# Group 0's first q and k loaded as FP32 by SyncE and cast on ScalarE and VectorE, with the first pass laid out anew

## The chip, the cores and the metric

The kernel runs on one core of a Trainium2 chip. The metric is the device time of one execution in microseconds. The engines are called as in the profile: PE (TensorE, matrix products), PEld (its weight loads), DVE (VectorE), ACT (ScalarE), POOL (GpSimd) and SP (SyncE). Loads and stores are DMA transfers. POOL and SP each issue them on a queue of their own; a load that changes the type on its way (FP32 in the chip's main memory, FP16 in its on-chip memory) is issued by POOL.

## The reference

Sigmoid attention, followed by a gated two-layer network without a bias:

```python
batch, n_heads, seq, head_dim = (8, 12, 448, 64)
scores = scale * np.matmul(q, k.transpose(0, 1, 3, 2)) - np.log(S)
attn = 1.0 / (1.0 + np.exp(-scores))
attn_out = np.matmul(attn, v)
...
x = attn_out.transpose(0, 2, 1, 3).reshape(B * S, H * D)     # 3584 x 768
h = x @ w_in                                                # 768 x 2048
g = h * (1.0 / (1.0 + np.exp(-beta * h)))
return (g @ w_out)                                          # 2048 x 768
```

q, k and v are FP32, as are the weights and the output.

## The kernel before, in words

**Groups.** Four heads of one batch make a group: 24 groups, three to a batch (`QPB`). For a group, `load_one` (L122) brings q or k into a tile `raw` of 128 partitions (32 for each head) with 14 chunks of 64 elements per partition, as FP16. `transpose` (L201) turns it on DVE into `qT` (L207) or `kT` (L216 for 12 chunks, L220 for the last two). There are three `raw` tiles, so the loads of group 3 write where group 0 was.

**Attention.** `score` (L230) is a matmul of 32 rows; two of them (e = 0, 1) accumulate a piece of the scores in PSUM. For batch 0 the scores are made in half visits (`half_visit`, L294): 224 query columns, with the key tiles 0 and 1 (`second` = 0) or 2 and the rest (`second` = 1). A visit writes two score tiles, and there are three of those in rotation (`share_psum(3)`), two pairs later on. ACT takes the sigmoid (L249, or L264 for two tiles in one instruction) into `attns`. `attend` (L316) multiplies with v (L334) and DVE casts the result into `xT` (L343). The v rows beyond the third key tile are loaded on their own (`load_v_last`) and copied once on DVE for the other half of the heads (`double_v_last`, L171).

**Network.** `dense1` multiplies batch 0 and 1 with w_in (L356), takes the sigmoid on ACT (L368) and the product on DVE into `gt` (L371), a tile of 128 x 16 x 896 FP16. `dense2` multiplies with w_out (L386). Later batches use products of sums of blocks (L510 and L628), which are not touched here.

**Order.** Each engine runs its instructions in the order in which the program writes them. The first pass (batch 0) is written out by hand: a list `LOADS` of loads on POOL's queue, a function `loads` with the ones after it, and a list `BEGIN` of steps: `q` and `k` are transposes, `scores` a half visit (group, half, second), `values` an `attend`, `dense` so many matmuls of the network (`fill_units`), `beta` four small transposes of beta, `idle` so many matmuls of a tile of zeros (`still`, L751), whose result nobody reads. `two` changes the score tiles from three pairs to two. After `BEGIN` a planner spreads the network's matmuls over the visits of the other groups.

**Start.** POOL issues the load of the first half of q of group 0 (chunks 0 to 6) and of its whole k, ahead of two small memsets; ACT runs a sigmoid of one column (`dummy`, L742) once its table is loaded; DVE sets `still` and `beta_in` to zero; PE runs 11 zero matmuls; SP issues the small load of beta (L766); POOL goes on with `LOADS`.

Of the kernel before, what the change touches and what calls it, by code (L numbers as in the profile page):

```python
# [8 lines left out]
FP32 = mybir.dt.float32  # L9
FP16 = mybir.dt.float16  # L10
# [3 lines left out]
def kernel(  # L14
# [10 lines left out]
    nc = tc.nc  # L25
# [3 lines left out]
    B, H, S, D = q.shape  # L29
    NTOK, DM = out.shape  # L30
    DFF = moe_w_in.shape[1]
    P = 128
    BLK = 32
    HQ = P // BLK
    NB = S // BLK
# [19 lines left out]
    rawp = ctx.enter_context(tc.tile_pool(name="rawp", bufs=3))  # L55
# [29 lines left out]
    def bank(cols: int = S, hold=None, at=None):  # L85
        if at is None:
            at = min((i for i in used if i not in held.values()), key=used.get)
        assert at not in held.values()
        touch(at)
        if hold is not None:  # L90
            held[hold] = at
        width[at] = cols
        return ps[:, at, 0:cols]
# [25 lines left out]
    raws = {}  # L119
    vs = {}  # L120

    def load_one(g: int, r: int, c0: int = 0, c1: int = NB):  # L122
        b, t = divmod(g, QPB)
        if g not in raws:
            raws[g] = rawp.tile([P, 2, NB, D], FP16, tag="raw", name="raw")
        nc.gpsimd.dma_start(  # L126
            out=raws[g][:, r, c0:c1].rearrange("p c d -> p (c d)"),
            in_=(q, k)[r][b, HQ * t : HQ * (t + 1)].rearrange("h (p c) d -> (h p) (c d)", c=NB)[
                :, c0 * D : c1 * D
            ],  # L130
        )

    def load_qk(g: int):
        load_one(g, 0)
        load_one(g, 1)
# [7 lines left out]
    def load_v_full(b: int, lo: int = 0, hi: int = H):  # L143

        if b not in vs:
            vs[b] = vp.tile([P, H, JF + 1, D], FP16, tag="v16", name="v16")
        rows = v[b, lo:hi].rearrange("h (p c) d -> p h (c d)", c=NB)
        for i in range(HQ):
            nc.gpsimd.dma_start(
                out=vs[b][i * BLK : (i + 1) * BLK, lo:hi, 0:JF].rearrange("p h j d -> p h (j d)"),  # L150
                in_=rows[:, :, JF * i * D : JF * (i + 1) * D],
            )
            ready.update((b, "full", t, i) for t in range(lo // HQ, hi // HQ))

    def load_v_last(b: int):
        if b not in vs:
            vs[b] = vp.tile([P, H, JF + 1, D], FP16, tag="v16", name="v16")
        rows = v[b].rearrange("h (p c) d -> p h c d", c=NB)
        for c in range(NF, NB):
            lo = (c - NF) * BLK  # L160
            nc.gpsimd.dma_start(out=vs[b][lo : lo + BLK, :, JF], in_=rows[:, :, c])
        ready.add((b, "last"))

    def load_v(b: int):
        load_v_full(b)
        load_v_last(b)

    def double_v_last(b: int):
        assert (b, "last") in ready
        ready.add((b, "v"))  # L170
        nc.vector.tensor_copy(out=vs[b][KL:P, :, JF], in_=vs[b][0:KL, :, JF])  # L171
# [3 lines left out]
    def load_w_in(lo: int, hi: int):  # L175

        nc.gpsimd.dma_start(
            out=w_in16[:, :, lo * P : hi * P],
            in_=moe_w_in[:, lo * P : hi * P].rearrange("(c p) f -> p c f", p=P),
        )  # L180

    def load_w_out(c: int, half: int):
        n = NDC // WOUT
        cols = slice(half * HALF, (half + 1) * HALF)
        nc.gpsimd.dma_start(
            out=w_out16[:, c * n : (c + 1) * n, cols],
            in_=moe_w_out[c * n * P : (c + 1) * n * P, cols].rearrange("(c p) f -> p c f", p=P),
        )
# [5 lines left out]
    ready = set()  # L194


    def in_order(b: int, t):
        t = t.rearrange("p c e -> p (c e)").bitcast(FP32)
        return t.rearrange("p (q c) -> p c q", c=NB) if b == B - 1 else t

    def transpose(g: int, r: int, c0: int = 0, c1: int = NB):  # L201
        raw = raws[g][:, r]
        if r == 0:
            if g not in qT:
                qT[g] = qTp.tile([P, NB * BLK, PAIR], FP16, tag="qT", name="qT")
            ready.update((g, "q", c) for c in range(c0, c1, NB // 2))
            nc.vector.transpose(  # L207
                out=in_order(g // QPB, qT[g][:, c0 * BLK : c1 * BLK]),
                in_=raw[:, c0:c1].rearrange("p c d -> p (c d)").bitcast(FP32),
            )  # L210
            return
        ready.add((g, "k"))
        kT[g] = kTp.tile([P, S, PAIR], FP16, tag="kT", name="kT")
        to = kT[g].rearrange("p k e -> p (k e)").bitcast(FP32)
        frm = raw.rearrange("p c d -> p (c d)").bitcast(FP32).rearrange("p (c f) -> p c f", c=NB)
        nc.vector.transpose(  # L216
            out=to[:, 0 : JF * P].rearrange("p (j i q) -> p i j q", j=JF, i=HQ),
            in_=frm[:, 0:NF].rearrange("p (i j) f -> p i j f", j=JF),
        )
        nc.vector.transpose(  # L220
            out=to[:, JF * P :], in_=frm[:, NF:].rearrange("p c f -> p (c f)")
        )
# [123 lines left out]
    gt = const.tile([P, NDC, WIN], FP16, name="gt")  # L346
# [388 lines left out]
    NH = NB // 2  # L735
    share_psum(3)
    with tc.manual_schedule():
        load_one(0, 0, 0, NH)
        load_one(0, 1)
        nc.gpsimd.memset(nlogs, NEG_LOG_S)  # L740
        nc.gpsimd.memset(dummy, 0.0)
        nc.scalar.activation(out=dummy, in_=dummy, func=AF.Sigmoid, bias=0.0, scale=1.0)  # L742
# [4 lines left out]
        idle = bank(512)  # L747

        def idle_units(n: int):
            for _ in range(n):  # L750
                nc.tensor.matmul(idle, still[:, 0:P], still, start=True, stop=True)  # L751

        idle_units(11)
        def load(what, *a):
            if what == "q":
                load_one(a[0], 0, a[1] * NH, (a[1] + 1) * NH)
            elif what == "k":
                load_one(a[0], 1)
            elif what == "v":
                load_v_full(0, a[0] * HQ, a[1] * HQ)  # L760
            elif what == "last":
                load_v_last(0)
            elif what == "w_in":
                load_w_in(*a)

        nc.sync.dma_start(out=beta_in[0:NDC], in_=moe_beta.rearrange("(c p) -> c p", p=P))  # L766
        LOADS = [
            ("q", 1, 0), ("k", 1), ("q", 2, 0), ("k", 2), ("last",), ("v", 0, 3), ("q", 0, 1), ("q", 1, 1),
            ("w_in", 0, 2), ("w_in", 2, 4), ("q", 2, 1), ("w_in", 4, 6), ("w_in", 6, 8), ("w_in", 8, 10),
            ("w_in", 10, 12), ("w_in", 12, 14), ("w_in", 14, 16),  # L770
        ]
        for x in LOADS:
            load(*x)

        def loads():
            load_qk(3)
            load_w_out(0, 0)
            load_w_out(1, 0)
            load_v(1)
            load_qk(4)  # L780
            load_qk(5)
            load_w_out(0, 1)
            load_w_out(1, 1)

        def beta_columns():
            ready.add("beta")
# [2 lines left out]
                nc.vector.transpose(out=beta_sb[part], in_=beta_in[:, part])  # L789

        BEGIN = [
            ("q", 0, 0), ("k", 0), ("q", 1, 0), ("scores", 0, 0, 1), ("idle", 4), ("k", 1), ("idle", 4),
            ("scores", 0, 0, 0), ("k", 2), ("q", 2, 0), ("scores", 1, 0, 0), ("idle", 4), ("v", 0),
            ("scores", 1, 0, 1), ("scores", 2, 0, 0), ("values", 0, 0), ("q", 0, 1), ("q", 1, 1),
            ("scores", 2, 0, 1), ("beta",), ("values", 1, 0), ("scores", 0, 1, 0), ("values", 2, 0),
            ("scores", 0, 1, 1), ("loads",), ("q", 2, 1), ("dense", 12), ("scores", 1, 1, 1), ("two",),
            ("dense", 6), ("scores", 1, 1, 0), ("dense", 18), ("scores", 2, 1, 0), ("values", 0, 1),
            ("values", 1, 1), ("scores", 2, 1, 1), ("dense", 9), ("values", 2, 1), ("dense", 42), ("k", 3),
            ("q", 3, 0), ("q", 3, 1), ("dense", 21),
        ]  # L800
        for what, *a in BEGIN:
            if what == "q":
                g, half = a
                transpose(g, 0, half * NH, (half + 1) * NH)
            elif what == "k":
                transpose(a[0], 1)
            elif what == "scores":
                half_visit(a[0], a[1] * QH, a[2])
            elif what == "idle":
                idle_units(a[0])  # L810
            elif what == "v":
                double_v_last(a[0])
            elif what == "values":
                attend(a[0], a[1] * QH, QH, a[2:] or (0, 1))
            elif what == "dense":
                fill_units(a[0])
            elif what == "beta":
                beta_columns()
            elif what == "loads":
                loads()  # L820
            elif what == "two":
                share_psum(2)
# [143 lines left out]
```

## Time and profile before

Three runs took 376.13, 376.32 and 376.49 us.

| | us |
|---|---|
| median of the runs | 376.32 |
| the profiled execution's own time | 376.51 |
| its span, first to last instruction | 374.7 |
| PE busy | 366.1 |
| ACT busy | 255.0 |
| DVE busy | 254.6 |
| POOL busy | 91.4 |
| first sigmoid of the scores begins | 7.38 |
| second visit's sigmoids begin | 9.71 |
| last sigmoid of batch 0's scores ends | 30.77 |
| PE's first long stretch of one line (L356) begins | 31.33 |

How to read the rows: a row of the chain of waits has its start and its length in us, the engine or the DMA, the tile and the line. A row of the timeline has the start, the time from the first to the last instruction of the row, the engine, the line, the operation, what it writes and reads, and how often; in brackets stands how long the engine had been idle before, and what ended that. A row of the DMA view has the tile, the issuing queue, the number of transfers, the KB written by each, and the median us from issue to landing. PEld, PE and the other engines count from the same zero.

### The profile page before, as it was taken

How to read it: one execution, taken by the hardware profiler on the slowest of the kernel's cores; microseconds unless marked ns; L12 is line 12 of the kernel's file. 1: busy time of each engine (PE TensorE's matmuls, PEld its weight loads, DVE VectorE, ACT ScalarE, POOL GpSimd, SP SyncE). 2: the span in 40 equal slices, each digit the busy share in tenths (PEclk: the TensorE clock that was granted, in tenths of full speed). 3: DMA queues.
4: the chain of work that ended last, by engine and by line, in shares of the span. 5: the costliest groups of instructions: out<-in, count | busy, mean ns of one | idle time of the engine just before them, and what ended most of it. 6: DMA issues, size and time to landing. Idle time of an engine off the chain costs nothing.

```text
span 374.7 us, 7249 instructions
## 1 busy us (share of the span) xinstructions
PE 366.1 (98%) x2871; PEld 181.8 (49%) x2871; DVE 254.6 (68%) x479; ACT 255.0 (68%) x293; POOL 91.4 (24%) x138
## 2 busy tenths in 40 slices
PE   8799999999999999999999999999999999999996
PEld 2466644444444455544444445554444455555653
DVE  2444796766686876787677667778766657679662
ACT  3995866698976658877767749887677737883000
POOL 8833353151151012325123003235100002230000
PEclk9999999999999999999999999999999999999999
DMA  8999999992359030039839311018903031000333
GB/s 116 184 197 203 197 204 199 221 124 51 49 73 182 5 86 1 0 51 125 171 49 207 88 26 29 0 32 112 166 2 84 13 74 42 1 2 1 86 84 126
DMA packets 42401, 34.29 MB, mean 92 GB/s; under 512 B 21872, under 2 KB 38912, under 8 KB 42368
## 3 DMA queue, kind: packets, MB, share of 16 engines
q0 software_dynamic: 36976, 22.81, 44.5%
q1 hardware_dynamic: 5392, 11.02, 10.4%
q8 instruction: 22, 0.36, 0.4%
q14 instruction: 11, 0.09, 0.1%
HBM read 45.62 MB, written 11.01 MB: 151 GB/s over the span
## 4 chain that ended last, share of the span: by engine, by line
PE 91%; ACT 5%; DMA 1%; issue 1%; DVE 0%; POOL 0%; ACTq 0%; POOLq 0%
PE ps L628 27%; PE ps L510 26%; PE ps L236 12%; PE ps L334 9%; PE ps L356 9%; PE ps L386 4%; PE ps L424 4%; ACT attns L249 3%; ACT attns L264 2%; DMA raw<-in_k_dram 1%; ACT sg L368 1%; PE ps L751 0%; POOL raw L126 0%; DVE kT L216 0%; DVE osb L401 0%
## 5 line engine op out<-in xcount | busy, mean ns | idle before, releaser
L264 ACT ACTIVATE attns<-ps,nlogs 128x1792 f16<-128x1792 f32 x75 | 131.6, 1754 | 47.1 <-PE ps L236 46.9
L524 POOL TENSOR_TENSOR gt<-attns,sg 128x448 f16<-128x448 f32 x21 | 23.9, 1137 | 141.5 <-ACT sg L521 141.5
L628 PEld LDWEIGHTS <-sum 128*128 128x128 f16 x440 | 40.0, 98 | 37.6 <-issue 12.8
L236 PE MATMUL ps<-qT,kT 32*128 32x448 f16 (+3 forms) x864 | 51.7, 339 | 3.3 <-ACT attns L249 1.8
L521 ACT ACTIVATE sg<-ps,beta_sb 128x448 f32<-128x448 f32 x72 | 45.1, 631 | 8.3 <-PE ps L510 5.8
L510 PE MATMUL ps<-xT,w_in 128*128 128x448 f16 x216 | 49.2, 353 | 0.0
L510 PE MATMUL ps<-xT,w_S 128*128 128x448 f16 x216 | 49.2, 352 | 0.0
L628 PE MATMUL ps<-w_T,sum 128*128 128x384 f16 x264 | 49.0, 327 | 0.0
L524 DVE TENSOR_TENSOR gt<-ps,sg 128x448 f16<-128x448 f32 x72 | 44.3, 619 | 3.9 <-ACT sg L521 3.7
L343 DVE CAST xT<-ps 128x448 f16<-128x448 f32 (+1 forms) x54 | 29.0, 570 | 20.1 <-PE ps L334 19.8
L646 DVE TENSOR_TENSOR osb<-ps,osb 128x384 f32<-128x384 f32 x55 | 30.5, 555 | 15.4 <-PE ps L628 13.5
L510 PEld LDWEIGHTS <-w_in 128*128 128x128 f16 x288 | 28.0, 98 | 26.6 <-issue 0.7
L334 PE MATMUL ps<-attns,v 128*64 128x448 f16 (+3 forms) x432 | 40.6, 340 | 0.1
L356 PE MATMUL ps<-xT,w_in 128*128 128x448 f16 (+1 forms) x240 | 39.4, 316 | 0.6 <-DVE gt L371 0.6
L617 DVE TENSOR_TENSOR sum<-gt 128x1024 f16<-128x1024 f16 x55 | 36.4, 679 | 0.2
L126 POOL DMA_DIRECT2D raw<-in_q_dram x27 | 15.1, 557 | 83.1 <-DVE kT L220 75.3
L371 DVE TENSOR_TENSOR gt<-ps,sg 128x448 f16<-128x448 f32 (+1 forms) x40 | 19.8, 527 | 21.2 <-ACT sg L368 21.0
L628 PE MATMUL ps<-w_out,gt 128*128 128x384 f16 x176 | 33.3, 327 | 0.0
L628 PE MATMUL ps<-w_out,sum 128*128 128x384 f16 x176 | 32.3, 327 | 0.0
L236 PEld LDWEIGHTS <-kT 32*128 32x128 f16 (+1 forms) x864 | 15.3, 96 | 32.2 <-issue 27.5
L570 DVE TENSOR_TENSOR ps<-ps,attns 128x448 f32<-128x448 f32 x24 | 15.2, 633 | 22.7 <-PE ps L510 22.7
L510 PEld LDWEIGHTS <-w_S 128*128 128x128 f16 x216 | 21.1, 98 | 19.4
(50 smaller groups left out, 376.0 us busy)
## 6 DMA issues: line engine op xcount, KB each, us to landing
out_dram<-osb SPq DMA_DIRECT2D x98, 96.0 KB, 1.9
raw<-in_k_dram POOLq DMA_DIRECT2D x24, 224.0 KB, 5.1
raw<-in_q_dram POOLq DMA_DIRECT2D x21, 224.0 KB, 3.9
v<-in_v_dram POOLq DMA_DIRECT2D x32, 144.0 KB, 6.1
w_in<-in_moe_w_in_dram POOLq DMA_DIRECT2D x8, 384.0 KB, 10.9
w_out<-in_moe_w_out_dram POOLq DMA_DIRECT2D x4, 768.0 KB, 13.9
v<-in_v_dram POOLq DMA_DIRECT2D x16, 48.0 KB, 6.0
out_dram<-osb SPq DMA_DIRECT2D x2, 384.0 KB, 2.3
```

The lines of the kernel that those rows point to most:

```text
L236: nc.tensor.matmul(sco[base : base + nk, hh, u0 : u0 + n], kT[g][lo : lo + BLK, jt * P : jt * P + nk, e], qT[g][lo : lo + BLK, c0 : c0 + n ...
L264: nc.scalar.activation(out=attns[:, slot : slot + 2].rearrange("p n h s -> p (n h) s"), in_=sco, func=AF.Sigmoid, bias=nlogs[:, 0:1], scal ...
L334: nc.tensor.matmul(av[hh * D : (hh + 1) * D, 0:n], vs[b][base : base + nk, 2 * (s % NPAIR) + hh, jt], at[base : base + nk, hh, 0:n], start ...
L343: nc.vector.tensor_copy(out=xTs[b][:, s % NPAIR, c0 : c0 + n], in_=av[:, 0:n])
L356: nc.tensor.matmul(m1, w_in16[:, hc, dc * P : (dc + 1) * P], xTs[b][:, hc, c0 : c0 + n], start=(hc == 0), stop=(hc == NHC - 1),)
L371: nc.vector.tensor_tensor(out=gt[:, dc, off : off + n], in0=m1, in1=sg[:, 0:n], op=ALU.mult)
L510: nc.tensor.matmul(out, w[:, c, i * P : (i + 1) * P], m[:, c], start=(start and c == 0), stop=(c == KH - 1), skip_group_check=not start,)
L521: nc.scalar.activation(out=sg, in_=h, func=AF.Sigmoid, bias=0.0, scale=beta_sb[:, dc : dc + 1])
L524: return lambda: engine.tensor_tensor(out=gt[:, dc, b % 2 * S : b % 2 * S + S], in0=h, in1=sg, op=ALU.mult)
L617: nc.vector.tensor_tensor(out=sums[t, i], in0=x, in1=y, op=op)
L628: nc.tensor.matmul(m2, (x if op is None else sums[t, i])[:, dc], w[:, dc], start=first, stop=(dc == ND - 1), skip_group_check=i >= 4,)
L646: nc.vector.tensor_tensor(out=out, in0=in0, in1=in1, op=op)
```

## The change

The load of the first half of q of group 0, and that of its k, leave POOL's queue. SP issues them as plain FP32 transfers into `staged`, the first four of the 16 columns of `gt` read as FP32 (k in the first 896 elements of each partition, q in the 448 after them). `gt` gets its first value of the network later. Casts into the usual `raw` tile follow as steps of `BEGIN`: seven chunks of q on ACT, eight chunks of k on DVE, six on ACT. The transposes read `raw` as before.

POOL's memsets now stand ahead of its loads, and `LOADS` begins with k, then q of group 1. The four `v` loads go ahead of the two of `last`; the second halves of q come in the order of groups 2, 1, 0, and all ahead of w_in. The later loads have another order as well (`LATER`), and their step stands behind the values of group 0's second half.

On PE the first 11 zero matmuls become 8, and those after them (4, 4, 4) become 3, 5 and 3 at other places. The visit of group 1 (`scores`, 1, 0, 0) goes ahead of that of group 0 (`scores`, 0, 0, 0). The transpose of q of group 2's second half moves from before the first network matmuls to after the visit (1, 1, 0). The other steps keep their order.

```diff
     def transpose(g: int, r: int, c0: int = 0, c1: int = NB):
         raw = raws[g][:, r]
+        assert g or (r, c0) == (0, NB // 2) or all((r, "cast", c) in ready for c in range(c0, c1))
...
-        load_one(0, 0, 0, NH)
-        load_one(0, 1)
-        nc.gpsimd.memset(nlogs, NEG_LOG_S)
...
-        idle_units(11)
...
         LOADS = [
-            ("q", 1, 0), ("k", 1), ("q", 2, 0), ("k", 2), ("last",), ("v", 0, 3), ("q", 0, 1), ("q", 1, 1),
-            ("w_in", 0, 2), ("w_in", 2, 4), ("q", 2, 1), ("w_in", 4, 6), ("w_in", 6, 8), ("w_in", 8, 10),
+            ("k", 1), ("q", 1, 0), ("q", 2, 0), ("k", 2), ("v", 0, 3), ("last",), ("q", 2, 1), ("q", 1, 1),
+            ("q", 0, 1), ("w_in", 0, 2), ("w_in", 2, 4), ("w_in", 4, 6), ("w_in", 6, 8), ("w_in", 8, 10),
             ("w_in", 10, 12), ("w_in", 12, 14), ("w_in", 14, 16),
         ]
+        LATER = [
+            ("qk", 3), ("w_out", 0, 0), ("qk", 4), ("w_out", 1, 0), ("values", 1), ("qk", 5), ("w_out", 0, 1),
+            ("w_out", 1, 1),
+        ]
+        staged = gt[:, 0:4].rearrange("p c w -> p (c w)").bitcast(FP32)
+        raws[0] = rawp.tile([P, 2, NB, D], FP16, tag="raw", name="raw")
+        parts = {0: (staged[:, NB * D :], NH), 1: (staged, NB)}
+        for r, (to, n) in parts.items():
+            nc.sync.dma_start(
+                out=to[:, 0 : n * D],
+                in_=(q, k)[r][0, 0:HQ].rearrange("h (p c) d -> (h p) (c d)", c=NB)[:, 0 : n * D],
+            )
+
+        def cast(r: int, c0: int, c1: int, act: bool):
+            out = raws[0][:, r, c0:c1].rearrange("p c d -> p (c d)")
+            frm = parts[r][0][:, c0 * D : c1 * D]
+            if act:
+                nc.scalar.copy(out=out, in_=frm)
+            else:
+                nc.vector.tensor_copy(out=out, in_=frm)
+            ready.update((r, "cast", c) for c in range(c0, c1))
+
+        nc.gpsimd.memset(nlogs, NEG_LOG_S)
...
         def loads():
-            load_qk(3)
-            load_w_out(0, 0)
-            load_w_out(1, 0)
-            load_v(1)
-            load_qk(4)
-            load_qk(5)
-            load_w_out(0, 1)
-            load_w_out(1, 1)
+            for x in LATER:
+                load(*x)
...
         BEGIN = [
-            ("q", 0, 0), ("k", 0), ("q", 1, 0), ("scores", 0, 0, 1), ("idle", 4), ("k", 1), ("idle", 4),
-            ("scores", 0, 0, 0), ("k", 2), ("q", 2, 0), ("scores", 1, 0, 0), ("idle", 4), ("v", 0),
-            ("scores", 1, 0, 1), ("scores", 2, 0, 0), ("values", 0, 0), ("q", 0, 1), ("q", 1, 1),
-            ("scores", 2, 0, 1), ("beta",), ("values", 1, 0), ("scores", 0, 1, 0), ("values", 2, 0),
-            ("scores", 0, 1, 1), ("loads",), ("q", 2, 1), ("dense", 12), ("scores", 1, 1, 1), ("two",),
-            ("dense", 6), ("scores", 1, 1, 0), ("dense", 18), ("scores", 2, 1, 0), ("values", 0, 1),
-            ("values", 1, 1), ("scores", 2, 1, 1), ("dense", 9), ("values", 2, 1), ("dense", 42), ("k", 3),
-            ("q", 3, 0), ("q", 3, 1), ("dense", 21),
+            ("idle", 8), ("cast", 0, 0, 7, True), ("q", 0, 0), ("cast", 1, 0, 8, False),
+            ("cast", 1, 8, 14, True), ("k", 0), ("q", 1, 0), ("scores", 0, 0, 1), ("k", 1), ("scores", 1, 0, 0),
+            ("idle", 3), ("scores", 0, 0, 0), ("k", 2), ("q", 2, 0), ("idle", 5), ("v", 0), ("scores", 1, 0, 1),
+            ("idle", 3), ("scores", 2, 0, 0), ("values", 0, 0), ("q", 0, 1), ("q", 1, 1), ("scores", 2, 0, 1),
+            ("beta",), ("values", 1, 0), ("scores", 0, 1, 0), ("values", 2, 0), ("scores", 0, 1, 1),
+            ("dense", 12), ("scores", 1, 1, 1), ("two",), ("dense", 6), ("scores", 1, 1, 0), ("q", 2, 1),
+            ("dense", 18), ("scores", 2, 1, 0), ("values", 0, 1), ("loads",), ("values", 1, 1),
+            ("scores", 2, 1, 1), ("dense", 9), ("values", 2, 1), ("dense", 42), ("k", 3), ("q", 3, 0),
+            ("q", 3, 1), ("dense", 21),
         ]
```

More of the change, by code (lines that the diff above doesn't have):

```diff
@@ L737, with load @@
     with tc.manual_schedule():
-        load_one(0, 0, 0, NH)
-        load_one(0, 1)
+        def load(what, *a):
+            if what == "q":
+                load_one(a[0], 0, a[1] * NH, (a[1] + 1) * NH)
+            elif what == "k":
+                load_one(a[0], 1)
+            elif what == "qk":
+                load_qk(a[0])
+            elif what == "v":
+                load_v_full(0, a[0] * HQ, a[1] * HQ)
+            elif what == "last":
+                load_v_last(0)
+            elif what == "values":
+                load_v(a[0])
+            elif what == "w_in":
+                load_w_in(*a)
+            elif what == "w_out":
+                load_w_out(*a)
+        LOADS = [
+            ("k", 1), ("q", 1, 0), ("q", 2, 0), ("k", 2), ("v", 0, 3), ("last",), ("q", 2, 1), ("q", 1, 1),
+            ("q", 0, 1), ("w_in", 0, 2), ("w_in", 2, 4), ("w_in", 4, 6), ("w_in", 6, 8), ("w_in", 8, 10),
+            ("w_in", 10, 12), ("w_in", 12, 14), ("w_in", 14, 16),
+        ]
+        LATER = [
+            ("qk", 3), ("w_out", 0, 0), ("qk", 4), ("w_out", 1, 0), ("values", 1), ("qk", 5), ("w_out", 0, 1),
+            ("w_out", 1, 1),
+        ]
+        staged = gt[:, 0:4].rearrange("p c w -> p (c w)").bitcast(FP32)
[14 more added lines that the diff above has]
+            ready.update((r, "cast", c) for c in range(c0, c1))
         nc.gpsimd.memset(nlogs, NEG_LOG_S)
@@ L751, in idle_units @@
                 nc.tensor.matmul(idle, still[:, 0:P], still, start=True, stop=True)
-        idle_units(11)
[L754 to L764, printed above, removed]
-        nc.sync.dma_start(out=beta_in[0:NDC], in_=moe_beta.rearrange("(c p) -> c p", p=P))
-        LOADS = [
-            ("q", 1, 0), ("k", 1), ("q", 2, 0), ("k", 2), ("last",), ("v", 0, 3), ("q", 0, 1), ("q", 1, 1),
-            ("w_in", 0, 2), ("w_in", 2, 4), ("q", 2, 1), ("w_in", 4, 6), ("w_in", 6, 8), ("w_in", 8, 10),
-            ("w_in", 10, 12), ("w_in", 12, 14), ("w_in", 14, 16),
-        ]
+        nc.sync.dma_start(out=beta_in[0:NDC], in_=moe_beta.rearrange("(c p) -> c p", p=P))
         for x in LOADS:
@@ L808 @@
                 half_visit(a[0], a[1] * QH, a[2])
+            elif what == "cast":
+                cast(*a)
             elif what == "idle":
```

## The prediction

> **What bounds the kernel now.** I read the page first, then the chain of waits in order of time, then the timeline of the first 12 us, engine by engine, then the stages by DMA rate and the time that each load took to land. From the page:
>
> ```profile
> span 374.7 us, 7249 instructions
> PE 366.1 (98%) x2871; PEld 181.8 (49%) x2871; DVE 254.6 (68%) x479; ACT 255.0 (68%) x293; POOL 91.4 (24%) x138
> PE 91%; ACT 5%; DMA 1%; issue 1%; DVE 0%; POOL 0%; ACTq 0%; POOLq 0%
> ```
>
> PE is the bound over the whole, but a busy PE says little of the start, since matmuls of zeros (L751) count as busy. The chain of waits shows what the start hangs on:
>
> ```profile
> 1.23 0.71 POOL raw L126
> 1.94 4.02 DMA raw<-in_k_dram
> 5.99 0.59 DVE kT L216
> 6.63 0.70 PE ps L236 x15
> 7.33 1.83 PE ps L751 x8
> ...
> 9.73 4.60 ACT attns L249 x5
> ...
> 30.83 0.51 PE ps L334 x6
> 31.33 9.53 PE ps L356 x63
> ```
>
> The load of k of group 0 ends at 5.96, its transpose at 6.58, then come the first scores. From 9.73 the chain runs through ACT, back and forth with the short matmuls that feed it, to 30.8; from 31.33 it is PE alone. So until 31 the sigmoids of the first pass set the time, and what counts is when ACT begins and whether it pauses:
>
> ```profile
> 7.38 1.53 ACT L249 ACTIVATE attns<-ps,nlogs 128x896 f16<-128x896 f32 x2 [4.52 <-PE ps L236]
> 9.71 4.61 ACT L249 ACTIVATE attns<-ps,nlogs 128x896 f16<-128x896 f32 x5 [0.80 <-PE ps L236]
> ```
>
> In brackets is ACT's idle time: 4.52 us before the first visit, 0.80 before the second; after that it is busy to 28.4. An unbroken chain would have begun at 9.71 - 1.53 = 8.18. That is the number to beat. The 0.80 is the matmuls waiting for k of group 1, whose transpose is the 8.12 row:
>
> ```profile
> 5.99 0.58 DVE L216 STREAM_TRANSPOSE kT<-raw 128x384 f32<-128x384 f32 x1 [1.65 <-DMA raw<-in_k_dram]
> 8.12 0.58 DVE L216 STREAM_TRANSPOSE kT<-raw 128x384 f32<-128x384 f32 x1 [0.88 <-DMA raw<-in_k_dram]
> 9.81 0.58 DVE L216 STREAM_TRANSPOSE kT<-raw 128x384 f32<-128x384 f32 x1 [0.99 <-DMA raw<-in_k_dram]
> ```
>
> All three k loads are waited for; the DMA engines set the pace of the start.
>
> **Loads of q and k of group 0.** Off POOL's queue: two issues (0.71 + 0.53 us). On SP's: the first half of q (224 KB as FP32), then k (448 KB), then beta's small load. SP is free at 0.7 (the beta issue at 1.29 had waited 0.6 for its memset, still so) and one issue took 0.40, so k goes out at 1.1. When does it land? The nearest rows are SP's stores:
>
> ```profile
> out_dram<-osb SPq DMA_DIRECT2D x8, 96.0 KB, 1.9
> out_dram<-osb SPq DMA_DIRECT2D x8, 96.0 KB, 4.0
> out_dram<-osb SPq DMA_DIRECT2D x2, 384.0 KB, 2.3
> ```
>
> The first is from a stretch without loads (281 to 286), the second from one with a q and a k load on POOL's queue (177 to 182), the third from the end. Alone, 448 KB costs about 2.5 by these, so 3.6 is the early bound for k. With POOL's loads beside it the second row adds 2.1, so 5.7. The late bound is the worst stretch (stores of 62 to 70, beside a full queue of w_out and v), up to 5.8 instead of 1.9: 3.6 + 3.9 = 7.5. Here SP's packets have a start: POOL's first packets came 1.2 us after the issue at 1.23, at 2.4. If the rest, 1.2 us of work, then has half of the engines, k lands at 4.8. I take 5.0, nearer to that than to 5.7, since POOL's backlog at that time is one load and not eight.
>
> **Casts.** q: 448 elements on ACT, about 0.53 (the L561 copy 128x448 takes 0.532). It lands about 2.7 and is cast and transposed by 3.7, under the wait for k. If that cover were gone it would cost 0.9. k: 384 elements on ACT 0.47 (the L649 copy 128x384 takes 0.474), beside 512 on DVE. DVE's nearest rows bound it: a CAST of 448 from PSUM takes 0.623, so 0.69 for 512; a copy of 768 f16 within SBUF takes 0.353. I take 0.5 for the pair. [...] No row here shows DVE reading FP32 from SBUF into f16. In both bounds the step stays between 0.47 and 0.69.
>
> **Sum for the first visit.** Before: the load lands at 5.96, ACT begins at 7.38: 1.42 between (kT 0.59, first scores, the start of ACT). After: 5.0 + 0.5 + 0.04 for the extra hand-over + 1.42 = 6.96. PE's 8 zero matmuls end at about 4.8, in front of that. The dummy sigmoid moves from 2.65 to about 2.0, as POOL's two memsets go ahead of its loads; these cost the loads 0.1.
>
> **Second visit.** It is now group 1, whose k and q are POOL's first loads (issue 1.3 and 1.9 instead of 3.06 and 2.54). Before, 1344 KB read had landed at 8.06. The same bytes are through by about 7.0: SP's start 0.8 us earlier, and engines that in the stretch from 4 to 6 moved only 123 GB/s, against 186 from 10 to 12, have two queues to draw on; the late bound is 8.06 - 0.3. DVE then needs 0.41 + 0.59 (q, k of group 1), so scores at 8.0, and ACT can go on at 8.4; its first visit lasts to 8.49. So the 0.80 pause is gone, just. In the late bound it stays at 0.6.
>
> **The chain from there.** ACT's effective start goes from 8.18 to 6.96: 1.2 us. Does something behind it come late? The third visit needs nothing new. k and q of group 2 landed by 9.8 and are wanted for the fifth visit (PE before: 14.37), so they have 3 us. v: the loads of "last" now follow the four of "full", and the DVE copy (0.35) waits for the latest. Before, the last v piece landed 5.7 after 8.38, at 14.1, because its issue was held 0.65 until a load eight places earlier (k of group 1) had landed; values of group 0 began at 14.87. After, that hold is earlier by a microsecond and more; the same bytes end about 12.6 and with the copy 13.0, wanted at 13.7. Cover 0.7. The second halves of q of groups 0 and 1 come behind q of group 2 now: 4032 KB read, against 3808 at 15.0 before, so some 14.4; wanted at 16.50 - 1.2 = 15.3. The transpose of q of group 2's second half moves behind two tensor products and the score visit; DVE had 1.4 to 1.6 us of idle time before each of those, it costs nothing, and 0.41 if that were full. The first two w_in pieces landed at 17.0 and 19.8, are wanted at 19.98 - 1.2 and 22.5 - 1.2, and come about a microsecond earlier: covered.
>
> **Later loads.** They now stand after the values of group 0's second half in the program. Group 3's q was issued at 20.36, just behind the DVE cast in front of it; at worst it now waits for the cast that ended at 28.05, so 26.9. At that time two w_in pieces of 2 us each are still on the way, so the DMA engines don't run dry. k of group 3 lands at about 33 (before 34.6), wanted at 38.69 - 1.2; w_out's first quarter at 37, wanted at 45.3; its next at 43.5, wanted at 47. If the moved issue really delayed them by its 6.5 us, k of group 3 would land at 41 and cost 3.6. I take nothing.
>
> **Sum.** Profiled execution: 376.51 (span 374.7, 1.8 around it) - 1.2 = 375.3. The median of the runs, 376.32, is 0.2 below the profiled one: 375.1.
>
> **Rivals.**
> - *The SP load is starved, and the kernel gets slower.* The place is k of group 0's landing; with ACT at landing + 1.96, the change breaks even at 6.2 and costs 0.75 from 7.0 on. For it: SP's stores took 5.1 to 5.8 instead of 1.9 beside deep POOL queues. Against it: that backlog was eight loads deep, and here SP begins first. At 7.5, ACT begins at 9.46: 1.3 slower, 377.6. Chance 0.18.
> - *The early bound.* POOL's first loads hardly disturb SP's, k lands at 3.6 to 4.3: gain 1.9 to 2.6 if group 1's loads keep up, 373.7 to 374.4. Chance 0.10.
> - *A slow TensorE.* The zero matmuls at the start began 0.43 us apart, and from 7.26 on eight took 1.83 us, 0.23 each: PE doubles its pace somewhere between, though the page's PEclk stays at full. The change cuts the first stretch from 11 to 8 (end 4.8, not 6.06) and leaves PE idle until 6.2. If PE then stays slow through the next visits, the zero matmuls written between them (3, 5, 3) cost 0.43 each, 1.3 + 2.1 + 1.3, in front of scores that ACT waits for. I count 0.6 for the fourth visit and 0.3 for the next: gain 0.3, 376.0. Chance 0.12. [...]
> - *Given back.* v, or the q halves, land after 14 and ACT pauses as long as it gained: 376.3. For it: v had 0.8 us to spare already. Against: all loads come earlier. Chance 0.08.
>
> **How the numbers follow.** The forecast (k lands at 4.3 to 5.6, gain 0.6 to 1.9, 374.4 to 375.7) has 0.52. About 0.2%, 0.75 us, is what measurement can tell here from no change. Faster by more: 0.50 of the forecast's and 0.10 of the early bound, 0.60. Within: the slow TensorE, the case of the gain given back and the forecast's edge, 0.22. Slower: 0.18. The range 374.0 to 377.2 leaves out part of the early bound (0.05) and about half of the starved load (0.10).
>
> **What would show it.** Right: k's SP load lands within about 4 us of its issue, two copies and a CAST of group 0 end before 5.7, the first sigmoid begins near 7.0 without the 0.80 pause behind it, and PE's unbroken stretch of L356 begins near 30.1 instead of 31.33. Wrong: a first sigmoid after 8.2; idle time of ACT between 9 and 20 that ends at L236 or L334; zero matmuls still 0.43 apart after 8 us; or PE waiting between 31 and 60 for group 3's k, w_out or v.

## The result and the profile after

The changed kernel takes 377.68 us (median of 22 runs, 375.28 to 378.69), the kernel before 376.30 (median of 22 beside it, 375.91 to 378.68): a ratio of 1.0032, 95% interval 1.0021 to 1.0042. It is slower by 1.2 to 1.4 us, where 1.2 us of gain was forecast. One run of the 22 took 375.28, about what was forecast; that it is alone is the clue to what follows. The profiled execution took 378.69, its span is 376.9.

The chain of waits of the changed kernel, for comparison with the one of before; columns are start, length, what:

```profile
8.15 1.00 PE ps L237 x14
9.15 1.40 PE ps L795 x3
11.41 2.25 PE ps L795 x5
14.50 1.01 ACT attns L250
...
32.52 9.53 PE ps L357 x63
```

PE's stretch of network matmuls begins at 32.52, not at 31.33: 1.19 late. L795 is the matmul of zeros, and it stands on the chain twice, for 1.40 and 2.25 us. ACT's timeline in the same kernel:

```profile
4.86 0.51 ACT L779 CAST raw<-gt 128x384 f16<-128x384 f32 x1 [0.86 <-DMA gt<-in_k_dram]
7.17 1.53 ACT L250 ACTIVATE attns<-ps,nlogs 128x896 f16<-128x896 f32 x2 [1.80 <-PE ps L237]
9.12 1.90 ACT L250 ACTIVATE attns<-ps,nlogs 128x896 f16<-128x896 f32 x2 [0.42 <-PE ps L237]
11.45 1.90 ACT L250 ACTIVATE attns<-ps,nlogs 128x896 f16<-128x896 f32 x2 [0.43 <-PE ps L237]
14.50 8.38 ACT L250 ACTIVATE attns<-ps,nlogs 128x896 f16<-128x896 f32 x10 [1.14 <-PE ps L237]
```

k of group 0 has landed by 4.86, where its casts begin (5.0 was forecast), and ACT begins earlier than before (7.17 against 7.38). But where it paused once (0.80), it now pauses three times, 1.99 us in all, each time for scores of PE. PE's timeline says why:

```profile
1.19 3.60 PE L795 MATMUL ps<-still 128*128 128x512 f16 x8 [1.19 <-DVE still L789]
6.04 1.07 PE L237 MATMUL ps<-qT,kT 32*128 32x224 f16 x16 [1.25 <-DVE kT L217]
8.15 1.00 PE L237 MATMUL ps<-qT,kT 32*128 32x224 f16 x16 [1.04 <-DVE kT L217]
9.08 1.46 PE L795 MATMUL ps<-still 128*128 128x512 f16 x3
10.48 0.93 PE L237 MATMUL ps<-qT,kT 32*128 32x224 f16 x16
11.34 2.32 PE L795 MATMUL ps<-still 128*128 128x512 f16 x5
13.59 0.85 PE L237 MATMUL ps<-qT,kT 32*128 32x224 f16 x16
14.38 0.82 PE L795 MATMUL ps<-still 128*128 128x512 f16 x3
```

Three zero matmuls take 1.46 at 9.08 and 0.82 at 14.38. Until about 14 PE works at half pace, and the zeros meant to fill its time stand in front of the scores. Before, the zeros from 7.26 on were already 0.23 apart. The profile's clock row shows full clock throughout both kernels all the same. The list of granted clocks that the trace keeps says why: its first entry, full clock, begins at 6.23 in the kernel before and at 13.97 in the changed one, and the row counts the time ahead of the first entry as full. There, only the spacing of the matmuls shows the half pace.

The rest of the loss can be followed by two landmarks, the start of the long stretch of L356 or L357 and the start of the last 32 matmuls (L424 or L425):

| kernel | long stretch | last 32 | between | from there to the end of the span |
|---|---|---|---|---|
| before | 31.33 | 366.14 | 334.81 | 8.6 |
| after | 32.52 | 367.95 | 335.43 | 8.9 |

1.19 us is lost in the start, 0.62 in between, 0.4 at the end. In the changed kernel's chain, DVE waits for a store that took 5.5 us to land beside loads, at 118 to 124; its wait for stores between 112 and 126 is 3.2 us, against 2.6 before, which is the 0.6. In the profiles of the eight experiments with the SP loads the middle is 334.8 to 335.3, in the three kernels with the old loads 334.8: so most of the 0.62 looks like that execution's own, a matter of how transfers meet in it. That is argued; no run isolates it.

### The profile page after: what moved, and what is told of

Read it like the earlier page. It is cut to its first block, busy times and chain, and to the rows that moved or that the text cites. A ratio compares the mean times of both kernels' runs of the same rounds, so it can differ in the third digit from the quotient of the medians.

```text
span 376.9 us, 7245 instructions
## 1 busy us (share of the span) xinstructions
PE 367.6 (98%) x2867; PEld 181.6 (48%) x2867; DVE 254.8 (68%) x480; ACT 256.3 (68%) x295; POOL 90.5 (24%) x136
## 4 chain that ended last, share of the span: by engine, by line
PE 88%; ACT 4%; DMA 3%; DVE 2%; issue 1%; SPq 0%; POOL 0%; DVEq 0%; ACTq 0%; POOLq 0%
PE ps L511 25%; PE ps L629 24%; PE ps L237 11%; PE ps L335 9%; PE ps L357 9%; PE ps L387 4%; PE ps L425 4%; ACT attns L250 2%; ACT attns L265 2%; DMA out_dram<-osb 1%; DMA raw<-in_q_dram 1%; PE ps L795 1%; DVE osb L647 1%; ACT sg L369 1%; DVE w_in L471 0%
## 5 line engine op out<-in xcount | busy, mean ns | idle before, releaser
L237 PE MATMUL ps<-qT,kT 32*128 32x448 f16 (+3 forms) x864 | 52.6, 347 | 3.3 <-DVE kT L217 2.3
L647 DVE TENSOR_TENSOR osb<-ps,osb 128x384 f32<-128x384 f32 x55 | 30.5, 555 | 15.4 <-PE ps L629 13.5
L357 PE MATMUL ps<-xT,w_in 128*128 128x448 f16 (+1 forms) x240 | 39.4, 316 | 0.6 <-DVE gt L372 0.6
L126 POOL DMA_DIRECT2D raw<-in_q_dram x26 | 14.3, 549 | 82.6 <-DVE kT L221 78.0
(52 smaller groups left out, 377.3 us busy)
```

The lines of the kernel that those rows point to most:

```text
L237: nc.tensor.matmul(sco[base : base + nk, hh, u0 : u0 + n], kT[g][lo : lo + BLK, jt * P : jt * P + nk, e], qT[g][lo : lo + BLK, c0 : c0 + n ...
L357: nc.tensor.matmul(m1, w_in16[:, hc, dc * P : (dc + 1) * P], xTs[b][:, hc, c0 : c0 + n], start=(hc == 0), stop=(hc == NHC - 1),)
L647: nc.vector.tensor_tensor(out=out, in0=in0, in1=in1, op=op)
```

## Experiments

**Theories.** A: PE is at half pace because it is idle from 4.8 to 6.04 (8 zeros instead of 11) and again from 7.1 to 8.15; the zeros behind cost double and delay scores. B: the loads are late (q of group 1 is transposed at 7.22, the copy of v waits until 13.84), and PE waits for them. Ten kernels were run; the kernel before ran beside each of them on the same chip, with medians of 376.34 to 376.50.

**1. Eleven zeros at the start again.**

```diff
-            ("idle", 8), ("cast", 0, 0, 7, True),
+            ("idle", 11), ("cast", 0, 0, 7, True),
```

> The changed kernel with 11 zero matmuls at the start instead of 8, as in the kernel before; nothing else. Theory A (TensorE stays at half its pace because the zero matmuls stop at 4.8 us and the next matmuls come at 6.04): the zero matmuls reach 6.06, the first score visit takes 0.57 to 0.70 instead of 1.07, those behind it as well, the zero matmuls between the visits are 0.23 apart, ACT's idle times of 0.43 and 1.14 before the third and fourth visits go, and the time falls to 375.0 to 375.6, with a narrow spread. Theory B (the loads are what is late: q of group 1 at 7.22, the last v pieces at 13.8): the time stays at 377 to 378, and ACT still pauses before the third or fourth visit.

376.91 median of 12 (375.83 to 379.26), ratio 1.0019 (1.0001 to 1.0037). The median misses the 375.0 to 375.6 expected of theory A, and its interval overlaps that of the change, so the times alone decide nothing. In the profiled execution, the fastest of the twelve, the matmuls do what the theory says:

```profile
6.14 0.70 PE L237 MATMUL ps<-qT,kT 32*128 32x224 f16 x16
8.09 0.58 PE L237 MATMUL ps<-qT,kT 32*128 32x224 f16 x16 [1.24 <-DVE kT L217]
8.60 0.82 PE L795 MATMUL ps<-still 128*128 128x512 f16 x3
...
10.26 1.25 PE L795 MATMUL ps<-still 128*128 128x512 f16 x5
```

```profile
8.70 11.99 ACT L250 ACTIVATE attns<-ps,nlogs 128x896 f16<-128x896 f32 x14 [0.27 <-PE ps L237]
```

The three zeros take 0.82, the five 1.25, ACT pauses for 0.27 only, and the long stretch begins at 30.34, 0.99 before the old one. B falls as the cause of the late third and fourth visits: with the same loads in the same order they come without a pause. It holds for the second visit, which still waits for group 1's transpose and so for its load, and costs ACT the 0.27. But the spread of 3.4 us was not forecast. The mean clock that the trace gives for each execution sorts it: the four runs at 1.000 took 375.83 to 376.38, the eight at 0.990 to 0.995 took 376.53 to 379.26. A clock of 0.995 is what one stretch of 3.41 us at half clock leaves over 375 us (experiment 2 shows such a stretch), 0.990 what two leave (experiment 4). So in the eight PE reached its full pace and lost it again. One hole is left that may cause it, PE's 1.24 us idle before 8.09.

**2. Eight zeros in the kernel before.**

```diff
-        idle_units(11)
+        idle_units(8)
```

> The kernel before with 8 zero matmuls at the start instead of 11; nothing else. Theory A: PE is idle from 4.8 to 6.63 and the next matmuls run at half pace; the eight zero matmuls behind the first visit take up to 3.4 us instead of 1.83, the next visit begins up to 1.6 later, and the time rises by 0.8 to 1.8 us, to 377.1 to 378.1. Theory B: the loads are as before, so the time stays at 376.3.

377.91 median of 12 (376.14 to 379.48), ratio 1.0024 (1.0003 to 1.0045). Three zeros fewer, and eight of twelve runs take 377.8 or more; the other four stay at 376.1 to 376.6. The profile shows PE falling back:

```profile
1.19 3.21 PE L751 MATMUL ps<-still 128*128 128x512 f16 x8 [1.19 <-DVE still L745]
6.50 0.70 PE L236 MATMUL ps<-qT,kT 32*128 32x224 f16 x16 [2.09 <-DVE kT L216]
7.13 3.46 PE L751 MATMUL ps<-still 128*128 128x512 f16 x8
```

The first eight end sooner than eight at 0.43 would (3.21, not 3.60), and the first visit takes 0.70: full pace was reached near the end. The trace's list of granted clocks says the same: full from 3.89 to 7.30, half from there to 10.72, then full again. After 2.09 us of idle time the next eight take 3.46 us, half pace, and the second visit waits for them: ACT's pause before it is 2.43 instead of 0.80.

**3. No zeros between the visits.**

```diff
-            ("idle", 3), ("scores", 0, 0, 0), ("k", 2), ("q", 2, 0), ("idle", 5), ("v", 0), ("scores", 1, 0, 1),
-            ("idle", 3), ("scores", 2, 0, 0),
+            ("scores", 0, 0, 0), ("k", 2), ("q", 2, 0), ("v", 0), ("scores", 1, 0, 1), ("scores", 2, 0, 0),
```

> The changed kernel without the zero matmuls between the visits (3, 5 and 3); the 8 at the start stay. Theory A: the matmuls stay at half pace for longer, but nothing stands in front of the scores that ACT waits for: the idle times of ACT before the third visit (0.43) and the fourth (1.14) go, the one before the second (0.42) stays; 376.0 to 376.6, unless the half pace lasts into the values and the network, where each visit or value product costs some 0.4 more and the time stays above 377. Theory B: unchanged at 377.7, since PE waits for loads and not behind its own zeros.

378.44 median of 5 (378.22 to 378.86), ratio 1.0050 (1.0038 to 1.0062): worse by the medians, and steadily so. The expected 376.0 to 376.6 was wrong, the clause behind it right: half pace now lasts into the values, where a product takes 1.67 instead of 0.99:

```profile
15.16 1.67 PE L335 MATMUL ps<-attns,v 128*64 128x224 f16 x16
...
20.17 0.99 PE L335 MATMUL ps<-attns,v 128*64 128x224 f16 x16
```

So the zeros do bring PE to its pace: in this profile the granted clock rises at 20.05, against 13.97 in the changed kernel.

**4. The later loads as before.**

```diff
-            ("beta",), ("values", 1, 0), ("scores", 0, 1, 0), ("values", 2, 0), ("scores", 0, 1, 1),
+            ("beta",), ("values", 1, 0), ("scores", 0, 1, 0), ("values", 2, 0), ("scores", 0, 1, 1), ("loads",),
...
-            ("dense", 18), ("scores", 2, 1, 0), ("values", 0, 1), ("loads",), ("values", 1, 1),
+            ("dense", 18), ("scores", 2, 1, 0), ("values", 0, 1), ("values", 1, 1),
```

(and `LATER` in its old order)

> The changed kernel with the later loads in their old order and at their old place (before the first network matmuls). Theory A: no effect on the first 33 us, 377.2 to 378.0. A third theory, C, that the new place and order of these loads causes the second part of the loss (0.6 us between 110 and 126 us in the profile): the time falls by about 0.6, to 377.0, and the stretch of matmuls after 126 us is 1.2 later than before the change and not 1.8.

378.01 median of 6 (376.89 to 378.60), ratio 1.0036 (1.0022 to 1.0049). Theory C falls: nothing is gained. The middle between the landmarks is 335.02 here. This profile also shows the second way to lose the pace: with the same 8 zeros the granted clock rose early, at 3.90, and fell to half from 7.32 to 14.14, over a hole of 2.14 us ahead of the second visit. Experiment 7's profile shows the same (full at 4.21, half from 7.62 to 14.45).

**5. Both holes filled.** As 1, and:

```diff
-            ("scores", 0, 0, 1), ("k", 1), ("scores", 1, 0, 0),
+            ("scores", 0, 0, 1), ("idle", 5), ("k", 1), ("scores", 1, 0, 0),
```

> The changed kernel with 11 zero matmuls at the start and 5 more between the first visit and the second (where PE was idle from 6.75 to 8.1). Theory A, in its second form (PE falls back to half pace when a stretch of some 3.4 us holds too little work, and the changed kernel has two holes in its first 8 us, not one): with both filled every run stays at full pace, the time is 375.4 to 376.2 with a spread below 1 us, and the runs of 377 to 379 that were left with 11 alone are gone. If the first hole were all, the spread of 375.8 to 379.3 would stay as it was with 11 alone.

375.96 median of 12 (375.44 to 377.26), ratio 0.9991 (0.9981 to 1.0002). All twelve have a clock of 0.998 or more, and ACT runs without a pause:

```profile
6.68 13.67 ACT L250 ACTIVATE attns<-ps,nlogs 128x896 f16<-128x896 f32 x16 [1.71 <-PE ps L237]
```

The runs of 378 and more are gone; two of twelve are at 376.9 and 377.3, so the spread is 1.8 and not below 1. Those two have a clock of 1.000, and what makes them late stays open. From 11 zeros to this, five matmuls whose results nobody reads take a microsecond off the median, though the two intervals just touch; from the change itself experiment 5 is clear.

**6. The SP loads alone.** The kernel before with `staged`, the two SP loads and the casts; its order and its zeros stay.

```diff
-        load_one(0, 0, 0, NH)
-        load_one(0, 1)
+        staged = gt[:, 0:4].rearrange("p c w -> p (c w)").bitcast(FP32)
...
-            ("q", 0, 0), ("k", 0), ("q", 1, 0), ("scores", 0, 0, 1), ("idle", 4), ("k", 1), ("idle", 4),
+            ("cast", 0, 0, 7, True), ("q", 0, 0), ("cast", 1, 0, 8, False),
+            ("cast", 1, 8, 14, True), ("k", 0), ("q", 1, 0), ("scores", 0, 0, 1), ("idle", 4), ("k", 1), ("idle", 4),
```

> The kernel before with the SP loads and the casts of group 0 alone; order of loads and steps and all zero matmuls (11, 4 + 4, 4) as before. k of group 0 lands near 4.9; the first visit begins behind the 11 zeros at 6.1, not 6.63; the second stands behind the 8 zeros and begins at 8.6, not 9.16, so that ACT's unbroken chain starts 0.5 earlier and the matmuls of L356 from 31.33 begin at 30.8. Theory A: no run falls back, and the time is 0.1 to 0.5 below that of the kernel before (0.5 less 0.4 for a longer end). Theory B (the loads cost more than they give): slower than before, because group 1's k or v comes late.

376.08 median of 11 (375.83 to 376.33), ratio 0.9989 (0.9980 to 0.9997): a small gain, with the narrowest spread of all. The first visit starts at 5.61 in the profiled execution, the second at 8.08, the long stretch at 30.31, a microsecond earlier than before, against 0.5 expected: the 11 zeros took 4.31 there and not 4.87, because full clock came sooner, at 4.80 instead of 6.23. That part is the luck of the profiled execution: the same 11 zeros took 4.87, 4.80, 4.55 and 4.76 in the profiles of experiments 1, 5, 8 and 10. ACT's pause before the second visit is 0.79, unchanged.

**7. Beta's load in seven.**

```diff
-        nc.sync.dma_start(out=beta_in[0:NDC], in_=moe_beta.rearrange("(c p) -> c p", p=P))
+        for lo, hi in ((0, 3), (3, 6), (6, 8), (8, 10), (10, 12), (12, 14), (14, 16)):
+            nc.sync.dma_start(out=beta_in[lo:hi], in_=moe_beta.rearrange("(c p) -> c p", p=P)[lo:hi])
```

> The changed kernel with beta's load cut in seven, which does nothing but raise the number of transfers on SP's queue from 106 to 112. In the profiles the time from PE's last 32 matmuls to the end of the span is 8.6 in the two kernels with 104 such transfers and 8.9 to 9.0 in the four with 106. They share eight semaphores in turn, and 104 and 112 are multiples of eight: if the last transfer's place in that turn sets how many waits follow it, the end is 8.6 here again; if the added casts or the loads lengthen it, 8.9 to 9.0.

One execution, span 376.7; from the last 32 matmuls (368.05) to the end 8.65. The end is short again. With 8.5 in experiment 8 (112 transfers too) and 8.9 to 9.0 in all seven profiles with 106, the end goes with the number of transfers on SP's queue and not with the loads or the casts, which are still there. In the traces of the two kernels the last store lands at 373.82 before the change and at 375.62 after it. Behind that, SP has one wait for a semaphore left in the kernel before (373.83) and seven in the changed one (375.63 to 376.00): about 0.37 of the 0.4. Whether the ends of the other kernels differ for the same reason was not shown.

**8. All mended.** As 1 and 7, and the second visit is group 0's:

```diff
-            ("scores", 0, 0, 1), ("k", 1), ("scores", 1, 0, 0),
-            ("idle", 3), ("scores", 0, 0, 0), ("k", 2),
+            ("scores", 0, 0, 1), ("idle", 4), ("scores", 0, 0, 0), ("k", 1),
+            ("idle", 3), ("scores", 1, 0, 0), ("k", 2),
```

> The changed kernel with 11 zeros at the start, the second visit that of group 0 (which needs no further load) behind 4 zeros, group 1's after 3 more, and beta's load in seven. By the sum of the prediction with the pause filled: ACT begins at 6.9 and runs on, 1.2 to 1.3 earlier than before, the matmuls of L357 begin near 30.1, the end has 8.6 again: 374.8 to 375.4, spread below 1 us, faster than both kernels. Theory B: ACT pauses later, for group 1 or for v, and the time is 376 or more.

375.31 median of 8 (374.92 to 376.02), ratio 0.9970 (0.9960 to 0.9981): faster than both kernels, with a spread of 1.1. ACT's row of the first pass and PE's in the chain of waits:

```profile
6.60 13.57 ACT L250 ACTIVATE attns<-ps,nlogs 128x896 f16<-128x896 f32 x16 [1.62 <-PE ps L237]
```

```profile
364.56 5.21 PE ps L425 x32
```

16 sigmoids without a gap from 6.60, the long stretch at 29.81, the last 32 matmuls 1.58 before the old ones.

**9. Only the second hole filled.** The five zeros of 5, with 8 at the start.

> The changed kernel with 8 zero matmuls at the start as it is, and 5 more between the first visit and the second: the second hole filled, the first (4.8 to about 5.9) left. With the first hole alone filled the runs spread from 375.8 to 379.3, with both filled from 375.4 to 377.3. If either hole by itself can drop PE to half pace, some runs here too have the 5 zeros 0.43 apart, the second visit at 9 instead of 8, and the median lies between 376.3 and 377.5 with runs up to 378. If the second hole is the cause and the first harmless, it is 375.9 with the narrow spread of the kernel with both filled.

376.96 median of 12 (375.81 to 377.34), ratio 1.0005 (0.9990 to 1.0020): by the medians a microsecond behind experiment 5, by the ratios half of that, and the intervals overlap. The profile says where the time goes:

```profile
6.93 2.31 PE L795 MATMUL ps<-still 128*128 128x512 f16 x5
9.83 11.99 ACT L250 ACTIVATE attns<-ps,nlogs 128x896 f16<-128x896 f32 x14 [1.24 <-PE ps L237]
```

Either hole is enough by itself, in its own way. With the second alone (experiment 1) PE reaches full pace and often loses it; with the first alone, here, no run has a clock below 0.998, but full pace comes late: the five zeros take 2.31 us in the profiled execution, half pace, ACT pauses for 1.24 before the second visit, and the granted clock rises at 9.30, not at 13.97. The slowest run is 1.3 us better than in the change; that the earlier rise is the reason is argued from the two profiles.

**10. The kernel before with four zeros instead of eight between the first two visits.**

```diff
-            ("scores", 0, 0, 1), ("idle", 4), ("k", 1), ("idle", 4),
+            ("scores", 0, 0, 1), ("idle", 4), ("k", 1),
```

> The kernel before with 4 zero matmuls between the first two visits instead of 4 + 4; its loads are untouched. The prediction read ACT's pause of 0.80 as a wait for group 1's k; the second visit there is group 0's own and needs no load, so the pause should be the 8 zeros in front of it. Then the second visit begins at 8.25 instead of 9.16, the pause goes, ACT's chain starts 0.8 earlier and the time is 375.5 to 375.8, without any change of the loads. If the pause was a wait for loads, it stays and the time stays 376.3; if four zeros are too few to keep the pace, some runs lie at 377 and more.

376.14 median of 12 (375.72 to 377.47), ratio 0.9992 (0.9976 to 1.0008): above the 375.5 to 375.8 expected, and no change by the times. The profile decides what it was run for:

```profile
7.19 8.68 ACT L249 ACTIVATE attns<-ps,nlogs 128x896 f16<-128x896 f32 x10 [4.33 <-PE ps L236]
16.26 5.14 ACT L249 ACTIVATE attns<-ps,nlogs 128x896 f16<-128x896 f32 x6 [0.38 <-PE ps L236]
```

```profile
14.59 0.99 PE L334 MATMUL ps<-attns,v 128*64 128x224 f16 x16 [0.57 <-DMA v<-in_v_dram]
```

The pause of 0.80 is gone with four zeros, and no load was touched. But then the values of group 0 wait 0.57 us for v, and ACT pauses for 0.38 later: the long stretch begins at 31.04, not at the 30.5 that 0.8 us would make. Here the loads do come to bind. Three runs of twelve, those with a clock of 0.995, took 376.95 to 377.47; none of the others more than 376.32.

## Why the prediction was wrong

**The step that failed** is TensorE's pace. The sum put it at nothing: the 1.42 us from k's landing to ACT, taken over from before, held first scores at full pace, and ACT was to run on from there. The rival "a slow TensorE" named the mechanism and the place (8 zeros instead of 11, PE idle until 6.2, the 3, 5 and 3 behind), but with a price of 0.6 + 0.3 = 0.9 us and a chance of 0.12. The price was 2.2 us in the profiles: with 11 zeros and PE at its pace the same kernel begins its long stretch at 30.34 (experiment 1), the changed one at 32.52. In the changed kernel's profile the first scores took 1.07 instead of 0.70, and ACT paused for 0.42, 0.43 and 1.14 before the second, third and fourth visits; of the 0.42, the 0.27 that experiment 1 keeps is group 1's load. Nor is it a rare case: of the 22 runs ten have a clock of 0.990 to 0.995, so that PE lost its pace, eleven have 0.998 or 0.999 and were late as well (the profiled one is of these, with its late rise at 13.97), and one, with 1.000, took 375.28. Experiment 2 shows that three zeros decide it in two runs of three. And the second hole, between the visits, was not seen at all: the prediction itself had computed scores at about 6.2 and 8.0, and did not ask what PE does in between.

**The pause of 0.80** was misread: "the matmuls waiting for k of group 1". The second visit of the kernel before is group 0's, which needs nothing new; the chain of waits shows 1.83 us of zero matmuls right in front of it, and experiment 10 takes the pause away by halving them. The change reversed the two visits, so that group 1's load stands in the way there: 8.15 for the second visit, where the four zeros of experiment 8 allow 7.45. The zeros that look like waste were in the kernel before what bridged both holes. And where the prediction had no pause left, 0.27 is there even with PE at its pace (experiment 1).

**What held.** k of group 0 landed by 4.86 (5.0 was taken; its casts begin at 4.4 to 5.0 in all nine profiles with the SP load), so the rival of the starved SP load is out. The casts took 0.56, 0.51 and 0.43 beside it, 0.54 from landing to transpose (0.5 was taken). DVE's cast of 512 took 0.43 (0.39 to 0.65 over the nine profiles), between the bounds of 0.353 and 0.69. Scores, values and loads behind held as well, where PE was at its pace: in experiment 1 the long stretch begins at 30.34, against the 30.1 that was forecast. v and group 3's loads cost nothing there. The copy of v waited until 13.84 in the change (13.0 was forecast), 0.8 late, in the shadow of PE's own delay.

**What was missing.** 0.4 us at the end for two more transfers on SP's queue. So even with PE at full pace the loads alone give 0.3 (experiment 6), since 0.4 of it is lost again; only experiment 8, 375.31, comes near 375.1, with the zeros, the visits and the transfers' number mended.

**The sum as it was.** The transpose of k begins at 5.40 instead of 5.99, -0.6; from there to ACT it is 1.77 instead of 1.39, +0.4, for the scores at half pace; so ACT starts 0.2 earlier. Its pauses are 1.99 instead of 0.80, +1.2. That makes 1.0 of the 1.19 at the long stretch. The last 0.2 lies inside ACT's rows: its first sixteen sigmoids take 13.71 without the pauses (1.53 + 1.90 + 1.90 + 8.38), and took 13.52 before (1.53 + 11.99). Then 0.6 in the middle and 0.4 at the end: 2.2, the two spans' difference. Of the 1.4 between the medians the end is 0.4, if it costs every run the same, which leaves about 1.0 for the start.

## What to carry to other kernels

Before a start-up is made shorter, count what PE does in every stretch of it: matmuls that nobody reads may be what keeps it at its pace, and a hole of 2.1 us was followed by double time for 3.4 us in experiment 2 and for 6.8 us in experiment 4; in the changed kernel everything up to 14 us ran at half pace. Read whether a pause is a wait for data or for instructions in front of it on the same engine; the chain of waits says it in its own lines. And look at the spread and the clock of each run, not only at the median, and at the spacing of equal matmuls besides, since the clock read full before the first rise. A kernel whose good runs are faster and whose usual runs are slower has its gain and its loss in different places.

## What the runs showed of the hardware

With 8 zero matmuls (3.2 to 3.6 us) and then 1.0 to 2.1 us of idle time PE was at half pace or fell back to it; with 11, and zeros in the hole behind the first visit (the kernel before, experiments 5, 6, 8 and 10), every profile shows full pace from 4.8 to 6.2 us on.

Between the changes of the granted clock that were read lay multiples of one time. In experiment 2 it was full for 3.41 us (3.89 to 7.30) and then at half for as long (to 10.72); in experiments 4 and 7 it stayed at half for 6.83 us. From its first rise to its fall at the end it was full for 368.64 us in the kernel before (6.23 to 374.87) and for 361.82 in the changed one (13.97 to 375.79), 108 and 106 times 3.413. Where the first rise falls differs from run to run: with 8 zeros at the start it came at 3.90 in experiment 4 and at 13.97 in the changed kernel, whose first visits are the same.

PE's busy time in single stretches of 3.41 us, counted from these changes: at half clock, 2.7 us in experiment 7 (7.62 to 11.03) with half clock after it, and 2.7 in experiment 2 (0.48 to 3.89) with full clock after it; at full clock, 1.3 in experiment 2 (3.89 to 7.30) with half clock after it, and 2.4 in the kernel before (9.64 to 13.06) with full clock after it. The ends of matmuls are modelled in a trace, and no experiment was made to find a limit.

The end of the kernel is 0.3 to 0.5 us longer with 106 transfers on SP's queue (8.9 to 9.0 us from the last 32 matmuls) than with 104 or 112 (8.5 to 8.7).
